# A weight decode of three vector operations instead of four, its low bits made on ScalarE, and a reordered start

## The chip, the core and the metric

One core of a Trainium2 chip runs the whole program. The metric is the device time of one execution in microseconds (us); the time of a kernel is the median of its runs. TensorE multiplies matrices, VectorE (DVE in the rows), ScalarE (ACT) and GpSimd (POOL) work element by element, and SyncE (SP) issues nearly all transfers. TensorE's clock has two levels, 1.2 and 2.4 GHz; the rows give the granted clock as a fraction of 2.4 GHz.

## The reference, cut to what matters

The program takes q, k and v of 4 batches, 8 heads, 576 positions and 64 channels. Each head gets two attentions: one over q, k and v averaged over groups of 4 positions, its result repeated 4 times, and one over the neighbours closer than 4 positions. Their sum, as 2304 tokens of 512 channels, goes through two feed-forward layers whose weights (512 x 2048 and 2048 x 512) come as 64-bit floats.

```python
out_d = sm_attn(q_d, k_d, v_d)             # q_d, k_d, v_d: means over 4 positions
out_up = np.repeat(out_d, factor, axis=2)
...
attn = attn / (np.sum(attn, axis=-1, keepdims=True) + 1e-09)   # masked to |i - j| < 4
out_local = np.matmul(attn, v)
return (out_up + out_local).astype(np.float32)
...
g = h * (1.0 / (1.0 + np.exp(-h)))         # first layer, h = x @ w_in; second: g = elu(h)
return (g @ w_out).astype(np.float32)
```

## The kernel before

**Attention.** Work goes in 16 pairs of heads, and the generator `attention(i)` issues the instructions of one pair piece by piece. A pair's q and k rows are transposed on TensorE (tile `pst`, line 276) and copied by ScalarE. VectorE sums them over groups of 4 (`qkD`, line 289). GpSimd sums the v rows over groups of 4 in three additions (`vt`, line 296, and `vd`, line 297). TensorE then makes the local scores (`psl`, line 308), VectorE adds the mask (line 315) and takes the maximum (`mx`, line 322), GpSimd subtracts it (line 323), ScalarE takes the exponential (line 353), VectorE sums, adds a small constant and inverts (`rl`, lines 355 to 357), and GpSimd multiplies (line 358). The averaged attention goes beside it (lines 334 to 363). Transposes (`aT`, `aD`), products with v (`psu`, `pso`) and a sum into `x32` (line 412) end the pair. The tiles `vt`, `E`, `aT` and `aD` share five buffers of one ring.

**Weights.** A weight tile of 128 x 512 values arrives as 128 x 1024 words in one of three `ws` buffers: the even words are the low halves of the 64-bit floats and the odd words the high halves. `magnitude` lets ScalarE take the absolute value of the high word, read as a float and scaled (line 147). `decode_w` then lets VectorE clamp it (line 156), shift out bits and sign (line 157), put the sign back (line 161) and put the top three bits of the low word into the last places (line 163), after which the next load goes to SyncE's queue (`load_next`). `split_w` makes a rounded high part on ScalarE (line 173) and the rest on GpSimd or VectorE (line 175). 64 weight tiles are decoded in all; the first 16 serve the first pass.

**Order.** Everything is written in one order by hand, and each engine runs its own instructions in that order. A first loop runs pairs 0 to 3 in turn, one piece a step (`step`), counting steps in `n`; in its later steps `small_first` puts in one piece of weight decoding a step, for at most `N_EARLY` = 9 tiles, up to three tiles in turn. The listing gives 82 steps. After it come the units of the matrix products: `g1` (tile `ph`, line 453) and `g2` (tile `y`, lines 504 and 506), with more pieces of attention and decoding at each `tick`; `need_first` forces the two weight tiles that a unit needs. TensorE's products use a high and a low part of both factors. Loads are issued first, in the order in which SyncE's queue runs them.

Of the kernel before, what the change touches and what calls it, by code (L numbers as in the profile page):

```python
# [9 lines left out]
F32 = mybir.dt.float32  # L10
F32R = mybir.dt.float32r
I32 = mybir.dt.int32
BF16 = mybir.dt.bfloat16
AF = mybir.ActivationFunctionType
ALU = mybir.AluOpType
# [6 lines left out]
def attention_moe_moe2_kernel(ctx, tc, q, k, v, wi1, wo1, wi2, wo2, out):  # L22
    nc = tc.nc
    B, H, S, D = q.shape
    NT, DM = out.shape
    DFF = wi1.shape[1]
    P = 128
    FAC = 4
    SD = S // FAC
    HS = SD // 2  # L30
    NPAIR = H // 2
# [12 lines left out]
    EPS = 1e-9  # L44
# [4 lines left out]
    N_EARLY = 9  # L49
# [5 lines left out]
    NW = 10  # L55
# [12 lines left out]
    cpool = ctx.enter_context(tc.tile_pool(name="cpool", bufs=1))  # L68
# [9 lines left out]
    att = attn_pools.enter_context(tc.tile_pool(name="att", bufs=2))  # L78
# [3 lines left out]

    ident = cpool.tile([P, P], F32, name="ident")
    mask = cpool.tile([P, NW // 2, WIN], F32, name="mask")

    def constants():
        make_identity(nc, ident)
        tmp = gp.tile([P, NBM], F32, tag="t", name="masktmp")[:, :4 * WIN].rearrange("p (n w) -> p n w", w=WIN)
        nc.gpsimd.memset(tmp, 0.0)
        for n, (half, low, high) in enumerate([(0, 0, 6), (0, -3, 3), (1, 0, 6), (1, -3, 3)]):  # L90

            for sign, bound in ((1, -low), (-1, high)):
                nc.gpsimd.affine_select(
                    out=tmp[:, n, :], in_=tmp[:, n, :], compare_op=ALU.is_ge, fill=MASKED,
                    base=bound + sign * WIN * half, pattern=[[sign, WIN]], channel_multiplier=-sign,
                )
        for s in range(NW // 2):
            nc.vector.tensor_copy(mask[0:WIN, s, :], tmp[0:WIN, 1 if s == 0 else 0, :])
            nc.vector.tensor_copy(mask[WIN:P, s, :], tmp[WIN:P, 3 if s == NW // 2 - 1 else 2, :])
# [19 lines left out]
    at = {"unit": 0, "load": 0, "decode": 0, "split": 0, "ahead": 2}  # L119

    def load_next():
        if at["load"] < len(order):
            load_w(at["load"])
            at["load"] += 1
# [17 lines left out]
    def magnitude(i):  # L142

        if i < len(order) and i not in wf:
            st = wst[i].rearrange("p (n w) -> p n w", w=2)
            t = wfp[-1].tile([P, DM], I32, tag="wf", name="wf", bufs=wf_bufs[-1])
            nc.scalar.activation(t.bitcast(F32), st[:, :, 1].bitcast(F32), AF.Abs, scale=65536.0)
            wf[i] = t

    def decode_w(i):  # L150
        magnitude(i)
        yield
        st = wst.pop(i).rearrange("p (n w) -> p n w", w=2)
        t = wf[i]
        tf = t.bitcast(F32)
        nc.vector.tensor_scalar(tf, tf, 2.0, W_MAX, op0=ALU.max, op1=ALU.min)  # L156
        nc.vector.tensor_scalar(t, t, 4, 1, op0=ALU.logical_shift_left, op1=ALU.logical_shift_right)  # L157
        yield
        if i + 1 - at["split"] < at["ahead"]:
            magnitude(i + 1)  # L160
        nc.vector.scalar_tensor_tensor(t, st[:, :, 1], -(1 << 31), t, op0=ALU.bitwise_and, op1=ALU.bitwise_or)  # L161
        yield
        nc.vector.scalar_tensor_tensor(t, st[:, :, 0], 29, t, op0=ALU.logical_shift_right, op1=ALU.bitwise_or)  # L163
        load_next()
        yield

# [14 lines left out]
    pairs = [(b, pr) for b in range(B) for pr in range(NPAIR)]  # L181
    loaded = {}
# [5 lines left out]
    def borrow(i, name):  # L188
        at, n = {"qk": (S, 2 * S), "qkD": (3 * S, 2 * SD), "vd": (3 * S + 2 * SD, 2 * SD)}[name]
        return x32[:, pairs[i][1], at:at + n][:, :2 * 2 * D if name == "vd" else n]  # L190

    def load_rows(i, which, engine=None):
        b, h0 = pairs[i][0], 2 * pairs[i][1]
        src = (q, k, v)[which]
        if which == 2:

            if i < NPAIR:
                heads = [wpool.tile([P, DM], F32R, tag=tag, name="rows2").bitcast(F32) for tag in ("wh0", "wl0")]
            else:
                t = nat.tile([P, 4 * FAC * D], F32, tag="natv", name="rows2", bufs=1)  # L200
                heads = [t[:, :DM], t[:, DM:]]
            for j, t in enumerate(heads):
                (engine or nc.sync).dma_start(t[:HS], src[b, h0 + j].rearrange("(p r) d -> p (r d)", r=2 * FAC))
            loaded[i, which] = heads
            return

        if i in (1, 2):
            t = xs.tile([P, KC * NBM], F32R, tag=("xh", "xl")[which], name=f"rows{which}").bitcast(F32)
            borrowed[2 * i - 2 + which] = t
        elif i == 3 and which == 0:  # L210
            borrowed["y"] = yp.tile([P, 4 * NBM], F32, tag="y", name="rows0")
            t = borrowed["y"]
        else:
            t = nat.tile([P, NTB * 2 * D], F32, tag="nat", name=f"rows{which}", bufs=2)
        t = t[:, :NTB * 2 * D].rearrange("p (c e) -> p c e", c=NTB)
        for j in range(2):
            (engine or nc.sync).dma_start(t[:TB, :, j * D:(j + 1) * D], src[b, h0 + j].rearrange("(c p) d -> p c d", p=TB))
        loaded[i, which] = t

    def load_windows(i):  # L220
        b, h0 = pairs[i][0], 2 * pairs[i][1]
        if i in (2, 3):
            vw = borrowed["y"][:, (i - 2) * NW * D:(i - 1) * NW * D].rearrange("p (n d) -> p n d", d=D)
        else:
            vw = nat.tile([P, NW, D], F32, tag="vw", name="vw")
        for j in range(2):
            rows = v[b, h0 + j]
            nc.sync.dma_start(
                vw[j * WIN:(j + 1) * WIN, :NW - 1, :],
                bass.AP(tensor=rows.tensor, offset=rows.offset, ap=[[D, WIN], [w0[1] * D, NW - 1], [1, D]]),  # L230
            )
            nc.sync.dma_start(vw[j * WIN:(j + 1) * WIN, NW - 1, :], rows[w0[-1]:w0[-1] + WIN, :])
        loaded[i, 3] = vw
# [6 lines left out]
    def load_pair(i):  # L240
        for which in range(3):
            load_rows(i, which)
# [15 lines left out]
    def ring(name, n):  # L258
        return att.tile([P, NW * WIN], F32, tag="ring", name=name, bufs=5)[:, :n]

    def attention(i):
# [11 lines left out]
        for parts in ([(0, c) for c in range(NTB - 1)], [(1, c) for c in range(NTB - 1)], [(0, NTB - 1), (1, NTB - 1)]):  # L273
# [3 lines left out]
            o = 0  # L277
            for which in range(2):
                n = TB * sum(w == which for w, _ in parts)
# [7 lines left out]
                    o += n  # L287
            yield
        nc.vector.reduce_sum(qkD, qk.rearrange("p (m r) -> p m r", r=FAC), axis=AX.X)

        vt = ring("vt", 2 * 2 * 2 * D).rearrange("p (n r d) -> p n r d", n=4, r=2)
        vd = borrow(i, "vd") if i < NPAIR else att.tile([P, 4 * D], F32, tag="vd", name="vd", bufs=2)
        vd = vd.rearrange("p (n d) -> p n d", n=4)
        for j, vn in enumerate(loaded.pop((i, 2))):
            vn = vn.rearrange("p (a r d) -> p a r d", a=2, r=FAC)
            nc.gpsimd.tensor_tensor(vt[:HS, 2 * j:2 * j + 2], vn[:HS, :, 0:2, :], vn[:HS, :, 2:4, :], ALU.add)
        nc.gpsimd.tensor_tensor(vd[:HS], vt[:HS, :, 0, :], vt[:HS, :, 1, :], ALU.add)
        if NPAIR - 1 <= i < len(pairs) - 1:
            load_pair(i + 1)
        qT, kT = tT  # L300
        qD, kD = tD

# [2 lines left out]
        for w in range(NW):  # L305
            o = (w % 2) * WIN
# [7 lines left out]
        for j in range(2):  # L314
            nc.vector.scalar_tensor_tensor(
                E[:, :, j, :], psl[j][:, :NW // 2 * WIN].rearrange("p (s w) -> p s w", w=WIN), BSCALE, mask,
                op0=ALU.mult, op1=ALU.add,
# [3 lines left out]
        mx = att.tile([P, NW, 1], F32, tag="mx", name="mx", bufs=4)  # L321
        nc.vector.tensor_reduce(mx, E3, axis=AX.X, op=ALU.max)
        nc.gpsimd.tensor_tensor(E3, E3, mx.to_broadcast([P, NW, WIN]), ALU.subtract)
        if i >= 2:
            load_windows(i)

# [3 lines left out]
        rl = att.tile([P, NW, 1], F32, tag="rl", name="rl", bufs=4)  # L330
# [22 lines left out]
        nc.scalar.activation(E3, E3, AF.Exp)  # L353
        yield
        nc.vector.reduce_sum(rl, E3, axis=AX.X)  # L355
        nc.vector.tensor_scalar_add(rl, rl, EPS)  # L356
        nc.vector.reciprocal(rl, rl)
        nc.gpsimd.tensor_tensor(E3, E3, rl.to_broadcast([P, NW, WIN]), ALU.mult)

# [174 lines left out]
    with tc.manual_schedule():  # L534
        for i in range(NPAIR):
            load_rows(i, 0)
            load_rows(i, 1, nc.scalar if i < 2 else nc.sync)
        for i in range(NPAIR):
            if i == 2:
                while at["load"] < 3:  # L540
                    load_next()
            load_rows(i, 2)
        load_windows(0)
        load_windows(1)

        zeros = gp.tile([P, NBM], F32, tag="t", name="zeros")
        nc.vector.memset(zeros, 0.0)
# [97 lines left out]
        while pending(0):  # L645
            step()

            while done < NPAIR and state["next"] > done and pairs[done] not in [p for p, _, _ in state["live"]]:
                next(first_x)
                done += 1  # L650
            n += 1
            if n <= 16:
                warm(1)
            if n > 36 and first["next"] < N_EARLY:
                small_first()
        del banks[1:]
        banks[0] = (ps_a, "a")
# [103 lines left out]
```

## Time and profile before

| | |
|---|---|
| median of 3 runs | 991.67 us (991.29 to 991.95) |
| the profiled execution | 991.21 us, its span 989.4 us |
| TensorE busy | 956.6 us (97%) |
| VectorE busy | 563.5 us (57%) |
| ScalarE busy | 412.4 us (42%) |
| GpSimd busy | 372.7 us (38%) |

The span runs from the first to the last instruction of the profiled execution. Busy time counts an instruction from its start to its end, so an instruction that has started and stands still counts as busy. Line numbers are those of the listing above. "Idle before" is the idle time of the engine just ahead of an instruction, and the arrow names what ended it.

### The profile page before, as it was taken

To read this page: it belongs to the slowest core of one execution; us is meant where nothing else is said; L and a number is where in the kernel's file an instruction comes from. 1 tells how busy PE (TensorE), PEld (TensorE's weight loads), DVE (VectorE), ACT (ScalarE), POOL (GpSimd) and SP (SyncE) were. 2 spreads that over 40 slices of the span, in tenths; PEclk is the share of its full clock that TensorE was granted. 3 is DMA by queue.
4 is the path that set the end of the run, shared out by engine and by line. 5 is a ranking of instruction groups with operands and counts; after the bars stand their busy time and mean duration, and the time that the engine had idled before them with its cause. 6 is when DMAs were issued, how large, how long until landed. Compare 5 with 4: busy or idle time off the path is not lost.

```text
span 989.4 us, 18693 instructions
## 1 busy us (share of the span) xinstructions
PE 956.6 (97%) x7453; PEld 884.8 (89%) x7453; DVE 563.5 (57%) x1012; ACT 412.4 (42%) x1032; POOL 372.7 (38%) x391
## 2 busy tenths in 40 slices
PE   7787799999999999999999999999999999999998
PEld 4566689999999999999999999999999999999997
DVE  6899955364479938766232367677644544334432
ACT  4455444545445456443333454433333433223321
POOL 4556755464422354222222362222223622222221
PEclk9758899999999999999999999999999999999999
DMA  9465553333125512434000101222000011101111
GB/s 219 106 167 134 155 129 75 97 84 89 36 86 162 167 57 86 129 109 127 23 22 24 43 1 54 86 96 64 33 33 32 1 64 65 63 2 64 64 36 60
DMA packets 90582, 77.74 MB, mean 79 GB/s; under 512 B 61568, under 2 KB 77952, under 8 KB 90496
## 3 DMA queue, kind: packets, MB, share of 16 engines
q1 hardware_dynamic: 88128, 75.97, 26.5%
q8 instruction: 58, 0.95, 0.4%
q10 hardware_dynamic: 2368, 0.59, 0.3%
q14 instruction: 28, 0.23, 0.1%
HBM read 62.39 MB, written 14.16 MB: 77 GB/s over the span
## 4 chain that ended last, share of the span: by engine, by line
PE 88%; DVE 8%; issue 1%; ACT 1%; DMA 1%; POOL 1%; SPq 0%; DVEq 0%; POOLq 0%; ACTq 0%
PE ph L453 41%; PE y L504 21%; PE y L506 20%; PE pso L404 2%; PE pst L276 1%; DVE wf L163 1%; DVE wf L161 1%; PE psu L392 1%; PE psl L308 1%; DVE wf L156 1%; PE psE L375 1%; PE psD L384 1%; DVE wf L157 1%; DVE rl L356 1%; DVE rl L355 1%
## 5 line engine op out<-in xcount | busy, mean ns | idle before, releaser
L476 POOL TENSOR_TENSOR gl<-t,gh 128x256 fp32r<-128x256 f32 (+1 forms) x240 | 218.0, 908 | 532.5 <-ACT gh L474 517.6
L453 PE MATMUL ph<-xl,wh 128*128 128x256 f32 (+1 forms) x960 | 278.6, 308 | 4.5 <-DVE xl L433 4.5
L453 PE MATMUL ph<-xh,wh 128*128 128x256 f32 (+1 forms) x960 | 278.6, 308 | 0.4 <-DVE t L466 0.4
L453 PEld LDWEIGHTS ph<-xl,wh 128*128 128x128 f32 x960 | 183.3, 191 | 9.7 <-DVE xl L433 4.9
L453 PEld LDWEIGHTS ph<-xh,wh 128*128 128x128 f32 x960 | 183.4, 191 | 7.0 <-issue 1.6
L453 PE MATMUL ph<-xh,wl 128*128 128x256 f32 (+1 forms) x960 | 178.6, 305 | 1.4 <-POOL wl L175 1.4
L504 PE MATMUL y<-gh,wh 128*128 128x256 f32 x576 | 168.9, 293 | 0.0
L474 ACT CAST gh<-t 128x256 fp32r<-128x256 f32 (+1 forms) x240 | 108.0, 450 | 139.6 <-DVE t L466 90.1
L504 PE MATMUL y<-gh,wl 128*128 128x256 f32 x576 | 164.5, 286 | 0.0
L504 PE MATMUL y<-gl,wh 128*128 128x256 f32 x576 | 164.5, 286 | 0.0
L466 DVE SCALAR_TENSOR_TENSOR t<-t,ph 128x256 f32<-128x256 f32 x144 | 60.3, 419 | 165.5 <-ACT t L464 165.5
L453 PEld LDWEIGHTS ph<-xh,wl 128*128 128x128 f32 x960 | 148.7, 191 | 2.3 <-POOL wl L175 1.6
L470 ACT ACTIVATE t<-t 128x384 f32<-128x384 f32 x96 | 50.4, 526 | 210.7 <-DVE t L469 210.7
L469 DVE TENSOR_SCALAR t<-ph 128x384 f32<-128x384 f32 x96 | 53.4, 556 | 125.6 <-PE ph L453 125.5
L506 PE MATMUL y<-wl,gh 128*128 128x512 f32 x288 | 113.9, 396 | 0.0
L464 ACT ACTIVATE t<-ph 128x256 f32<-128x256 f32 x144 | 55.3, 384 | 140.3 <-PE ph L453 131.5
L506 PE MATMUL y<-wh,gl 128*128 128x512 f32 x288 | 113.7, 395 | 0.0
L504 PEld LDWEIGHTS y<-gh,wh 128*128 128x128 f32 x576 | 111.8, 194 | 1.9 <-issue 1.0
L504 PEld LDWEIGHTS y<-gh,wl 128*128 128x128 f32 x576 | 112.0, 194 | 0.0
L504 PEld LDWEIGHTS y<-gl,wh 128*128 128x128 f32 x576 | 112.0, 194 | 0.0
L506 PE MATMUL y<-wh,gh 128*128 128x512 f32 x288 | 111.9, 389 | 0.0
L472 DVE SCALAR_TENSOR_TENSOR t<-t,ph 128x384 f32<-128x384 f32 x96 | 53.2, 554 | 56.8 <-ACT t L470 56.8
(85 smaller groups left out, 1241.8 us busy)
## 6 DMA issues: line engine op xcount, KB each, us to landing
ws<-in_moe_w_in_dram SPq DMA_DIRECT2D x32, 512.0 KB
ws<-in_moe_w_out_dram SPq DMA_DIRECT2D x32, 512.0 KB
rows<-in_v_dram SPq DMA_DIRECT2D x36, 144.0 KB
rows<-in_q_dram SPq DMA_DIRECT2D x32, 144.0 KB
yp<-yo SPq DMA_DIRECT2D x9, 512.0 KB
part<-yp SPq DMA_DIRECT2D x9, 512.0 KB
yp<-yo SPq DMA_DIRECT2D x6, 768.0 KB
part<-yp SPq DMA_DIRECT2D x6, 768.0 KB
```

What stands on the lines that cost most here:

```text
L156: nc.vector.tensor_scalar(tf, tf, 2.0, W_MAX, op0=ALU.max, op1=ALU.min)
L404: nc.tensor.matmul(ps[j * D:(j + 1) * D, o:o + n], loaded[i, 3][j * WIN:(j + 1) * WIN, w, :], aT[j * WIN:(j + 1) * WIN, w // 2, c0:c0 + n] ...
L453: nc.tensor.matmul(ph[:, :nb], a[:, c, :], b[:, c, :], start=k == 0, stop=k == 3 * KC - 1)
L464: nc.scalar.activation(t, h, AF.Tanh, scale=0.5)
L466: nc.vector.scalar_tensor_tensor(t, t, 1.0, h, op0=ALU.add, op1=ALU.mult)
L469: nc.vector.tensor_scalar_min(t, h, 0.0)
L470: nc.scalar.activation(t, t, AF.Exp)
L472: nc.vector.scalar_tensor_tensor(t, t, -1.0, h, op0=ALU.add, op1=ALU.max)
L474: nc.scalar.copy(gh, t)
L476: nc.gpsimd.tensor_tensor(gl, t, gh.bitcast(F32), ALU.subtract)
L504: nc.tensor.matmul(y[d // 2][:, h:h + nb], wm[:, sl], gm, start=first and d % 2 == 0, stop=last, skip_group_check=True)
L506: nc.tensor.matmul(y[d], gm[:, sl], wm, start=first, stop=last)
```

## The change

Five things are edited. ScalarE gets a second instruction for each weight tile, right behind the absolute value: it reads the low word as an unsigned integer, scales it by 2^-29 with an offset and writes the rounded result, the three bits, back over the low word. VectorE's shift becomes one operation that shifts the clamped value left by 3 and puts in these bits; the fourth operation goes, and with it one break (`yield`) in `decode_w`. The sums of v on GpSimd, and the loads of the next pair that follow them, move from ahead of the local scores to behind the subtraction of the maximum. The constant added to `rl` comes from a tile `eps` through a `tensor_tensor`. The first weight loads move ahead of the v rows, in turn with them and with the v windows, and the first loop begins to decode at every second step from step 13 on, where it was every step from step 37 on.

```diff
--- before.py
+++ after.py
@@ -10,6 +10,7 @@
 F32 = mybir.dt.float32
 F32R = mybir.dt.float32r
 I32 = mybir.dt.int32
+U32 = mybir.dt.uint32
 BF16 = mybir.dt.bfloat16
 AF = mybir.ActivationFunctionType
 ALU = mybir.AluOpType
@@ -82,9 +83,11 @@
 
     ident = cpool.tile([P, P], F32, name="ident")
     mask = cpool.tile([P, NW // 2, WIN], F32, name="mask")
+    eps = cpool.tile([P, 1], F32, name="eps")
 
     def constants():
         make_identity(nc, ident)
+        nc.gpsimd.memset(eps, EPS)
         tmp = gp.tile([P, NBM], F32, tag="t", name="masktmp")[:, :4 * WIN].rearrange("p (n w) -> p n w", w=WIN)
         nc.gpsimd.memset(tmp, 0.0)
         for n, (half, low, high) in enumerate([(0, 0, 6), (0, -3, 3), (1, 0, 6), (1, -3, 3)]):
@@ -145,6 +148,8 @@
             st = wst[i].rearrange("p (n w) -> p n w", w=2)
             t = wfp[-1].tile([P, DM], I32, tag="wf", name="wf", bufs=wf_bufs[-1])
             nc.scalar.activation(t.bitcast(F32), st[:, :, 1].bitcast(F32), AF.Abs, scale=65536.0)
+
+            nc.scalar.activation(st[:, :, 0].bitcast(U32), st[:, :, 0].bitcast(U32), AF.Copy, scale=2.0 ** -29, bias=2.0 ** -10 - 0.5)
             wf[i] = t
 
     def decode_w(i):
@@ -154,13 +159,11 @@
         t = wf[i]
         tf = t.bitcast(F32)
         nc.vector.tensor_scalar(tf, tf, 2.0, W_MAX, op0=ALU.max, op1=ALU.min)
-        nc.vector.tensor_scalar(t, t, 4, 1, op0=ALU.logical_shift_left, op1=ALU.logical_shift_right)
+        nc.vector.scalar_tensor_tensor(t, t, 3, st[:, :, 0], op0=ALU.logical_shift_left, op1=ALU.bitwise_or)
         yield
         if i + 1 - at["split"] < at["ahead"]:
             magnitude(i + 1)
         nc.vector.scalar_tensor_tensor(t, st[:, :, 1], -(1 << 31), t, op0=ALU.bitwise_and, op1=ALU.bitwise_or)
-        yield
-        nc.vector.scalar_tensor_tensor(t, st[:, :, 0], 29, t, op0=ALU.logical_shift_right, op1=ALU.bitwise_or)
         load_next()
         yield
 
@@ -287,16 +290,6 @@
                     o += n
             yield
         nc.vector.reduce_sum(qkD, qk.rearrange("p (m r) -> p m r", r=FAC), axis=AX.X)
-
-        vt = ring("vt", 2 * 2 * 2 * D).rearrange("p (n r d) -> p n r d", n=4, r=2)
-        vd = borrow(i, "vd") if i < NPAIR else att.tile([P, 4 * D], F32, tag="vd", name="vd", bufs=2)
-        vd = vd.rearrange("p (n d) -> p n d", n=4)
-        for j, vn in enumerate(loaded.pop((i, 2))):
-            vn = vn.rearrange("p (a r d) -> p a r d", a=2, r=FAC)
-            nc.gpsimd.tensor_tensor(vt[:HS, 2 * j:2 * j + 2], vn[:HS, :, 0:2, :], vn[:HS, :, 2:4, :], ALU.add)
-        nc.gpsimd.tensor_tensor(vd[:HS], vt[:HS, :, 0, :], vt[:HS, :, 1, :], ALU.add)
-        if NPAIR - 1 <= i < len(pairs) - 1:
-            load_pair(i + 1)
         qT, kT = tT
         qD, kD = tD
 
@@ -321,6 +314,16 @@
         mx = att.tile([P, NW, 1], F32, tag="mx", name="mx", bufs=4)
         nc.vector.tensor_reduce(mx, E3, axis=AX.X, op=ALU.max)
         nc.gpsimd.tensor_tensor(E3, E3, mx.to_broadcast([P, NW, WIN]), ALU.subtract)
+
+        vt = ring("vt", 2 * 2 * 2 * D).rearrange("p (n r d) -> p n r d", n=4, r=2)
+        vd = borrow(i, "vd") if i < NPAIR else att.tile([P, 4 * D], F32, tag="vd", name="vd", bufs=2)
+        vd = vd.rearrange("p (n d) -> p n d", n=4)
+        for j, vn in enumerate(loaded.pop((i, 2))):
+            vn = vn.rearrange("p (a r d) -> p a r d", a=2, r=FAC)
+            nc.gpsimd.tensor_tensor(vt[:HS, 2 * j:2 * j + 2], vn[:HS, :, 0:2, :], vn[:HS, :, 2:4, :], ALU.add)
+        nc.gpsimd.tensor_tensor(vd[:HS], vt[:HS, :, 0, :], vt[:HS, :, 1, :], ALU.add)
+        if NPAIR - 1 <= i < len(pairs) - 1:
+            load_pair(i + 1)
         if i >= 2:
             load_windows(i)
 
@@ -353,7 +356,7 @@
         nc.scalar.activation(E3, E3, AF.Exp)
         yield
         nc.vector.reduce_sum(rl, E3, axis=AX.X)
-        nc.vector.tensor_scalar_add(rl, rl, EPS)
+        nc.vector.tensor_tensor(rl, rl, eps.rearrange("p (n o) -> p n o", o=1).to_broadcast([P, NW, 1]), ALU.add)
         nc.vector.reciprocal(rl, rl)
         nc.gpsimd.tensor_tensor(E3, E3, rl.to_broadcast([P, NW, WIN]), ALU.mult)
 
@@ -535,13 +538,12 @@
         for i in range(NPAIR):
             load_rows(i, 0)
             load_rows(i, 1, nc.scalar if i < 2 else nc.sync)
+        load_next()
         for i in range(NPAIR):
-            if i == 2:
-                while at["load"] < 3:
-                    load_next()
             load_rows(i, 2)
-        load_windows(0)
-        load_windows(1)
+            if i < 2:
+                load_windows(i)
+                load_next()
 
         zeros = gp.tile([P, NBM], F32, tag="t", name="zeros")
         nc.vector.memset(zeros, 0.0)
@@ -651,7 +653,7 @@
             n += 1
             if n <= 16:
                 warm(1)
-            if n > 36 and first["next"] < N_EARLY:
+            if n > 12 and n % 2 and first["next"] < N_EARLY:
                 small_first()
         del banks[1:]
         banks[0] = (ps_a, "a")
```

## Rows read from the trace of the kernel before

**Rows 1.** Busy time by stretch: microseconds and instructions of each engine, granted clock, DMA.
```profile
0.00:34.00 34.00, 23.60 (x292) 14.16 (x293) 20.95 (x42) 13.78 (x47) 19.54 (x34) 0.97 0.92 199
34.00:70.00 36.00, 30.44 (x305) 22.04 (x302) 32.95 (x56) 18.70 (x50) 17.59 (x15) 0.59 0.48 128
70.00:130.00 60.00, 46.94 (x472) 41.37 (x472) 57.31 (x89) 31.60 (x94) 45.22 (x37) 0.84 0.64 156
130.00:990.00 860.00, 855.58 (x6389) 807.22 (x6388) 452.33 (x827) 348.28 (x843) 290.33 (x307) 1.00 0.21 66
```

**Rows 2.** Chain that ended last, shares by line: 53 to 64 us, 64 to 131 us.
```profile
by line: PE psu L392 23.2%; PE pso L404 22.8%; PE pst L276 17.4%; PE psE L375 13.9%; PE psD L384 11.6%; PE psl L308 11.4%; issue 0.4%
...
by line: DVE wf L163 13.7%; issue 12.2%; DVE wf L161 9.4%; DVE wf L156 8.5%; DVE xl L433 7.1%; DVE wf L157 4.9%; DVE E L315 4.5%; DVE mx L322 4.5%; DVE qkD L289 4.0%; DVE t L466 3.6%; DVE x L412 3.4%; DVE rl L355 3.3%; DVE nm L343 3.3%; ACT
```

**Rows 3.** Instructions by line, VectorE, first 130 us: count, busy, mean ns, idle before.
```profile
L163 DVE SCALAR_TENSOR_TENSOR wf<-ws,wf 128x512 int32<-128x512 int32 x16 | 16.3, 1029 | 0.0
L157 DVE TENSOR_SCALAR wf<-wf 128x512 int32<-128x512 int32 x16 | 15.3, 958 | 0.6
L161 DVE SCALAR_TENSOR_TENSOR wf<-ws,wf 128x512 int32<-128x512 int32 x16 | 14.6, 918 | 0.0
L156 DVE TENSOR_SCALAR wf<-wf 128x512 f32<-128x512 f32 x16 | 10.8, 674 | 6.3 <-ACT wf L147 6.3
...
L433 DVE TENSOR_TENSOR xl<-x,xh 128x256 fp32r<-128x256 f32 x8 | 6.3, 794 | 0.0
...
L356 DVE TENSOR_SCALAR rl<-rl 128x10 f32<-128x10 f32 x7 | 5.2, 747 | 0.2
```

**Rows 4.** Timeline, 28 to 60 us: start, length, engine, line; POOL is GpSimd.
```profile
35.11 0.43 DVE L157 TENSOR_SCALAR wf<-wf 128x512 int32<-128x512 int32 x1
35.57 0.69 DVE L161 SCALAR_TENSOR_TENSOR wf<-ws,wf 128x512 int32<-128x512 int32 x1
...
37.87 1.67 POOL L323 TENSOR_TENSOR E<-E,mx 128x640 f32<-128x640 f32 x1 [4.96 <-DVE mx L322]
...
38.45 1.37 DVE L157 TENSOR_SCALAR wf<-wf 128x512 int32<-128x512 int32 x1
```

**Rows 5.** Timeline, 126 to 131 us, one subtraction on VectorE among GpSimd instructions.
```profile
126.89 1.28 POOL L175 TENSOR_TENSOR wl<-wf,wh 128x512 fp32r<-128x512 f32 x1
126.94 2.77 DVE L433 TENSOR_TENSOR xl<-x,xh 128x256 fp32r<-128x256 f32 x1
...
128.14 1.25 POOL L323 TENSOR_TENSOR E<-E,mx 128x640 f32<-128x640 f32 x1
```

**Rows 6.** Busy time of the instructions on tile wf alone, two stretches.
```profile
34.00:70.00 36.00, 22.47 (x27) 9.06 (x14) 7.99 (x6) 0.59 0.48 128
70.00:130.00 60.00, 33.43 (x37) 11.24 (x18) 13.79 (x10) 0.84 0.64 156
```

**Rows 7.** Timeline of the first 30 us, the softmax of the first pairs.
```profile
9.78 0.82 DVE L322 TENSOR_REDUCE mx<-E 128x10 f32<-128x640 f32 x1
...
14.95 1.41 POOL L296 TENSOR_TENSOR vt<-rows 72x256 f32<-72x256 f32 x2 [11.25 <-DMA rows<-in_v_dram]
...
17.12 1.26 POOL L323 TENSOR_TENSOR E<-E,mx 128x640 f32<-128x640 f32 x1
...
18.41 0.74 ACT L353 ACTIVATE E<-E 128x640 f32<-128x640 f32 x1 [3.07 <-POOL E L323]
...
20.03 1.76 DVE L356 TENSOR_SCALAR rl<-rl 128x10 f32<-128x10 f32 x1
```

**Rows 8.** DMA of the first 60 us in 40 slices, rate of each.
```profile
GB/s 0 149 264 213 214 215 215 220 224 254 266 339 364 243 178 184 122 96 109 109 134 228 235 104 11 115 332 129 4 0 0 0 104 407 188 0 0 61 296 3
```

**Rows 9.** Waits of the first 130 us: in total, times, longest.
```profile
DVE wf L156 <- ACT wf L147: 6.3, 4, 3.8
ACT aD L385 <- POOL x L297: 6.2, 1, 6.2
```

**Rows 10.** Instructions by line, ScalarE, first 130 us.
```profile
L147 ACT ACTIVATE wf<-ws 128x512 f32<-128x512 f32 x16 | 10.8, 676 | 4.5 <-POOL wl L175 4.2 <-DMA ws<-in_moe_w_out_dram 0.3
```

## Prediction

> **What bounds the kernel now.** I read the busy times by stretch first [rows 1]. From 130 us on TensorE is busy for 855.58 of 860 us at a granted clock of 1.00, the 2.4 GHz level, and the few idle microseconds are the tail. Nothing that this change does can shorten that stretch, because the products in it stay the same. So the time is about 860 us plus the moment at which this regime begins, and the question is only how much earlier than 130 us that is. Before it TensorE has 10.4 idle us up to 34, 5.6 from 34 to 70 and 13.1 from 70 to 130, and its clock is 0.59 and 0.84 in the last two.
>
> Next is what those 130 us wait for. VectorE is busy for 32.95 of 36 and 57.31 of 60 us in the two later stretches [rows 1]. The chain that ended last [rows 2] runs from 64 to 131 us mostly through the decode's lines 163, 161, 156 and 157. Between 53 and 64 us, however, it is TensorE alone, with the attention's products at a clock of 0.5, the 1.2 GHz level.
>
> VectorE's busy time is not all work [rows 3, 4]. With GpSimd idle the shift took 0.43 us and the next operation 0.69 us. The shift at 38.45 us took 1.37 us: GpSimd's subtraction had begun at 37.87 us for 1.67 us, and the shift ended 0.28 us behind it. So this shift stands while GpSimd works, and its mean is 958 ns. The operations with two tensors do the same: at 126.94 us a `tensor_tensor` took 2.77 us, through two GpSimd instructions, and ended just behind the second [rows 5]. From 34 to 130 us the decode's 64 VectorE operations hold 55.9 us [rows 6], where their undisturbed lengths (two at 0.43, two at 0.69) come to 16 x 2.24 = 35.8 us. About 20 us are waiting, 0.31 us an operation.
>
> **The decode after the first loop.** Of the 64 operations 27 lie in 34 to 70 us and 37 in 70 to 130 us [rows 6]. A step of the first loop that decodes moves one of up to three tiles on by one piece, with seven pieces to a tile before and six after. Counting them through to step 82, the new order leaves 28 of 48 operations behind it, where the old left 37 of 64: the same share, so the same nine weight tiles are still to do. Nine operations go. Lower bound of the gain: the operation that goes is a shift in effect (one shift and one combination become one combination), 0.43 us undisturbed, and all the waiting moves to the other three, because GpSimd's work does not shrink: 9.25 x 0.43 = 4.0 us. Upper bound: each of the nine takes its full mean with it, 33.43 x 9/37 = 8.1 us. GpSimd is busy for 45.22 of the 60 us, so part of the waiting will come back. I take the middle, **6.0 us**.
>
> **The decode within the loop.** Steps 13 to 36 now hold eight decode operations that stood behind step 36; steps 37 to 82 hold 12 instead of 27. At the old mean (22.47/27 = 0.83 us) VectorE loses 12.5 us of its 32.95. The stage can't shrink by that: TensorE is idle for only 5.6 of its 36 us at this clock, and it is the chain for 11 us of it [rows 1, 2]. Bounds: 0 and 5.6 us at the same clock, more only if the clock rises. I take **5.0 us**, near the idle time, since the waits ahead of 53 us are VectorE's and GpSimd's.
>
> **The start.** Now GpSimd's first work is the first v sum at 14.95 us, behind an 11.25 us wait for v rows, and the first subtraction comes at 17.12 us, although its maximum was ready at 10.6 us; ScalarE's exponential waits 3.07 us for it [rows 7]. The move frees that subtraction. It does not free the second: in GpSimd's queue it stands behind the first v sum, and so do all the later ones. That v sum now waits longer, since one weight load of 0.52 MB passes the first v rows; at the 266 to 364 GB/s of the slices in which the loads ran [rows 8] this is 1.4 to 2.0 us. On ScalarE the absolute values of tiles 0, 1 and 2 stand at steps 13, 17 and 23, ahead of transposes and exponentials of pairs 1 to 3. The second load is queued behind 2.36 MB of q and k, the first load, one v pair (0.29 MB) and its windows (0.33 MB): 4.0 MB in all with itself; the slices sum to that at about 18.5 us, where ScalarE would come to it at about 17. The third needs 1.15 MB more, at about 23 us. What is queued behind each wait is all of ScalarE's attention work, and TensorE waits for its copies. Against this, VectorE is idle for 13 of the first 34 us [rows 1], so the eight operations (6.7 us at the old mean) find room there, though GpSimd's 19.54 busy us in this stretch will lengthen them [rows 1]. The ring helps: ScalarE waited 6.2 us for the last v sum before `aD` got its buffer [rows 9], and this v sum is now allocated later than that `aD`. Bounds: no loss, and 6 us (three stalls of 2 us). I take a loss of **2.5 us**.
>
> **ScalarE's new instruction.** No row shows it. Nearest is line 147, the same 128 x 512 with the same two-word stride, mean 676 ns [rows 10]. 16 of them cost ScalarE about 11 us in the first 130 us, where it is idle for about half. It is hidden by that, and by VectorE's clamp, which needs only the absolute value and runs 0.43 us meanwhile. Uncovered it costs its length wherever VectorE already waited for ScalarE: four times, 6.3 us in all [rows 9]. Bounds 0 and 4 x 0.68 = 2.7 us; I take **1.0 us**. Behind 130 us the 48 others are covered by TensorE.
>
> **The sum's constant.** Line 356 takes 747 ns on the mean over 10 elements, once 1.76 us [rows 3, 7]. As a `tensor_tensor` it reads two tensors, and rows 5 show such an operation standing behind GpSimd too. The Trainium skill, page "SBUF — State Buffer", section "Who interferes with whom", says that a VectorE instruction with two SBUF inputs contends with a GpSimd instruction that reads SBUF, and that only instructions with one input outside the two-port modes are free. By that rule this edit frees nothing, and the trace agrees with the 2.77 us of [rows 5]. Even if it did, line 360, a `tensor_scalar`, comes two instructions later. Bounds: 0, and 7 x 0.747 = 5.2 us if it came to cost nothing at all. I take **0**.
>
> **Loads later on.** The next pair's loads stand in SyncE's queue behind a later v sum, so a weight load behind them can come later by the two GpSimd instructions in between, some 2 us a pair. Weight loads wait for free buffers anyway; I take 0, at most 2 us.
>
> **Sum** against the profiled execution of 991.21 us: -6.0 - 5.0 + 2.5 + 1.0 = -7.5, or 983.7 us. The median is 0.46 us above that execution, so I predict **984.2 us**. A difference under 0.2% (2 us) can't be told from none here.
>
> **Rivals.** (1) *GpSimd sets the pace.* All waiting returns: 4.0 us after the loop, 7 x 0.43 = 3.0 within it, less 3.5: about 988.2 us. For it speaks GpSimd's 45.22 us; against it that this busy time also holds waiting for VectorE. (2) *The stages overlap better.* With VectorE light, TensorE stays busy, its clock rises in 34 to 70 us, and VectorE's whole 12.5 us count there for 9, with 8.1 after the loop and nothing lost at the start: about 975 us. Against it: that stage had a clock of 0.59. (3) *Slower: ScalarE stands at the loads.* If the waits at steps 17 and 23 last 6 to 7 us each (loads land late, as the first v rows did after 11.25 us of waiting), the start loses 13 instead of 2.5 us: 994.7 us. It decides from a start loss of 10 us on. Against it: the rates of [rows 8]. (4) *No change*: TensorE at the low clock holds 34 to 70 us and the start eats the rest: -4.0 + 3.5, about 991 us.
>
> **How the numbers follow.** My forecast (981 to 987.5 us) has 0.45, rival 1 (to 989.6) 0.13, rival 2 (below 981) 0.20, no change 0.08, slower 0.14. Faster: 0.45 + 0.13 + 0.20 = 0.78. The range 976 to 990.5 us leaves out the far end of rival 2, rival 3 and half of rival 4.
>
> **What would show it.** Right: TensorE's last long wait ends 6 to 9 us before 130 us; 48 VectorE decode operations for the first 16 tiles in about 45 us; ScalarE waits of about 2 us for `ws` at 15 to 25 us; line 356 still over 1 us where GpSimd works; the first subtraction near 11 us. Wrong: a first product of tile `ph` later than 68 us, a new ScalarE instruction above 1 us, or waits of VectorE for ScalarE well above 6.3 us.

## The result, and the profile after

The changed kernel takes 1001.87 us in the median (999.95 to 1004.7, four runs) against 991.48 us before: a ratio of 1.011, with a 95% interval of 1.0078 to 1.0142. It is slower, where 984.2 us was forecast and 976 to 990.5 us was the range. The slowest execution before (991.95 us) and the fastest after (999.95 us) lie 8 us apart. Its profiled execution took 1000.22 us, with a span of 998.4 us, 9.0 us above that of before.

Busy time by stretch of the kernel after, which answers to [rows 1]:

```profile
0.00:34.00 34.00, 24.53 (x282) 14.73 (x282) 23.07 (x41) 16.48 (x48) 17.20 (x30) 0.85 1.06 196
34.00:70.00 36.00, 27.24 (x312) 19.60 (x312) 30.35 (x50) 20.08 (x57) 19.06 (x18) 0.67 0.54 124
70.00:130.00 60.00, 43.81 (x430) 38.29 (x430) 47.58 (x71) 33.93 (x91) 39.03 (x34) 0.77 0.57 145
130.00:998.00 868.00, 860.91 (x6437) 810.92 (x6433) 434.96 (x789) 376.65 (x900) 300.82 (x313) 1.00 0.22 67
```

From 130 us on, TensorE is busy for 860.91 us where it was 855.58: 5.3 us more of its work is left at that moment. It is also idle for 7.1 us there, where it was 4.4. VectorE did get lighter, 47.58 instead of 57.31 us from 70 to 130, but TensorE was busy for 3.1 us less in that same stretch, with a granted clock of 0.77 where it had been 0.84. The engine that had been busiest there was relieved, and the work that counts fell behind.

The decode's part of these rows, by the instructions on tile `wf` alone (VectorE, ScalarE and GpSimd), answers to [rows 6]:

```profile
0.00:34.00 34.00, 8.97 (x8) 2.64 (x4) 1.46 (x1) 0.85 1.06 196
34.00:70.00 36.00, 12.16 (x13) 5.73 (x9) 5.07 (x4) 0.67 0.54 124
```

VectorE had no decode up to 34 us before. So its other work there fell from 20.95 to 23.07 - 8.97 = 14.10 us, and from 34 to 70 us it rose from 32.95 - 22.47 = 10.48 to 30.35 - 12.16 = 18.19 us. The early decode did not only fill idle time: it went in ahead of other work, which came later.

A marker for how far behind is ScalarE's sixteenth reading of `ph`. One instruction by its tile, before and then after; the last time in each line (169.6 and 173.9 us) is the start of the sixteenth:

```profile
L464 ACT ACTIVATE t<-ph x16: 372/384/402, 74.5 to 169.6; 128x256 f32<-128x256 f32 x16
```
```profile
L467 ACT ACTIVATE t<-ph x16: 377/385/413, 76.5 to 173.9; 128x256 f32<-128x256 f32 x16
```

So 4.3 of the 9.0 us are lost by this point, and the other 4.7 us behind it. Behind it TensorE has 5890 instructions (5891 before); it is idle for 7.5 us where it was 3.8, and busy for 817.03 us where it was 815.98. The idle part, 3.6 us, is TensorE's waits of the kernel after from 160 us on, which are new (before had 0.2 us in all there); the 1.1 us of longer busy time stay open:

```profile
PE pst L279 <- ACT ED L351: 1.4, 1, 1.4
PE ph L456 <- DVE t L469: 1.1, 1, 1.1
PE pst L279 <- DMA rows<-in_q_dram: 1.1, 1, 1.1
PE psu L395 <- ACT aD L388: 0.2, 1, 0.2
```

VectorE's instructions by line in the first 140 us, after, answering to [rows 3]:

```profile
L162 DVE SCALAR_TENSOR_TENSOR wf<-wf,ws 128x512 int32<-128x512 int32 x16 | 21.3, 1331 | 1.1
L166 DVE SCALAR_TENSOR_TENSOR wf<-ws,wf 128x512 int32<-128x512 int32 x16 | 16.2, 1018 | 0.0
L161 DVE TENSOR_SCALAR wf<-wf 128x512 f32<-128x512 f32 x16 | 13.6, 847 | 5.8 <-ACT wf L150 5.8
...
L363 DVE TENSOR_SCALAR sm<-sm 72x4 f32<-72x4 f32 x7 | 3.7, 527 | 0.0
L359 DVE TENSOR_TENSOR rl<-rl,eps 128x10 f32<-128x10 f32 x7 | 2.8, 400 | 0.2
```

The 48 operations take 51.1 us, where 64 took 57.0 and about 45 was forecast. Each that is left takes longer, the new L162 1331 ns on the mean. With the decode alone (*e1_decode*, below) the 48 take 45.0 us, as forecast, and the new operation 1071 ns.

ScalarE's two instructions for a tile, same stretch, answering to [rows 10]:

```profile
L150 ACT ACTIVATE wf<-ws 128x512 f32<-128x512 f32 x16 | 10.8, 674 | 7.2 <-DMA ws<-in_moe_w_in_dram 5.1 <-DMA ws<-in_moe_w_out_dram 2.1
L152 ACT ACTIVATE ws<-ws 128x512 uint32<-128x512 uint32 x16 | 10.6, 664 | 0.0
```

The new one takes 664 ns, as long as the row that bounded it. But ScalarE now stands 7.2 us for weight loads, where the old listing had 0.3.

Timeline of the kernel after, 10 to 30 us, answering to [rows 7]:

```profile
10.69 1.26 POOL L316 TENSOR_TENSOR E<-E,mx 128x640 f32<-128x640 f32 x1 [6.96 <-DVE mx L315]
...
17.32 0.72 POOL L323 TENSOR_TENSOR vt<-rows 72x256 f32<-72x256 f32 x1 [5.37 <-DMA rows<-in_v_dram]
18.13 0.66 ACT L150 ACTIVATE wf<-ws 128x512 f32<-128x512 f32 x1 [3.23 <-DMA ws<-in_moe_w_in_dram]
...
22.50 0.67 ACT L150 ACTIVATE wf<-ws 128x512 f32<-128x512 f32 x1 [2.07 <-DMA ws<-in_moe_w_out_dram]
...
28.00 0.68 ACT L150 ACTIVATE wf<-ws 128x512 f32<-128x512 f32 x1 [1.88 <-DMA ws<-in_moe_w_in_dram]
```

The first subtraction came at 10.69 us, as forecast. The first v sum came at 17.32 us, 2.4 us later than before, and the three waits of ScalarE for its loads are 3.23, 2.07 and 1.88 us.

Finally a wait that no row of before has. Timeline of the kernel after, 75 to 94 us (SPq is SyncE's queue):

```profile
75.91 0.51 SPq L139 DMA_DIRECT2D ws<-in_moe_w_out_dram  x1
...
84.99 0.40 SPq L134 DMA_DIRECT2D ws<-in_moe_w_in_dram  x1
...
86.38 0.92 SPq L220 DMA_DIRECT2D rows<-in_q_dram  x2
...
93.15 1.04 PE L279 MATMUL pst<-ident,rows 96*128 96x96 f32 x5 [4.88 <-DMA rows<-in_q_dram]
```

and the same pair's loads before:

```profile
71.70 0.36 SPq L136 DMA_DIRECT2D ws<-in_moe_w_out_dram  x1
77.03 0.40 SPq L131 DMA_DIRECT2D ws<-in_moe_w_in_dram  x1
77.55 0.97 SPq L217 DMA_DIRECT2D rows<-in_q_dram  x2
```

After, the queue stood with a weight load until 84.99 us, when a `ws` buffer came free, and the q rows were behind it and one more. They left 8.8 us later than before, and TensorE stood 4.88 us for them.

### The profile page after: what moved, and what is told of

It reads as the page before. It is cut to its first block, busy times and chain, and to the rows that moved or that the text cites. A ratio compares the mean times of both kernels' runs of the same rounds, so it can differ in the third digit from the quotient of the medians.

```text
span 998.4 us, 18706 instructions
## 1 busy us (share of the span) xinstructions
PE 956.5 (96%) x7453; PEld 883.5 (88%) x7453; DVE 536.0 (54%) x948; ACT 447.1 (45%) x1096; POOL 376.1 (38%) x392
## 4 chain that ended last, share of the span: by engine, by line
PE 65%; DMA 1%; DVE 0%; ACT 0%; issue 0%; SPq 0%
PE ph L456 33%; PE y L509 20%; PE y L507 13%; DMA ws<-in_moe_w_in_dram 0%; DMA ws<-in_moe_w_out_dram 0%; DVE part L530 0%; ACT ws L152 0%; DVE wf L166 0%; DVE wf L162 0%; ACT t L467 0%; DVE t L469 0%; DVE wf L161 0%; ACT wf L150 0%; SPq L134 0%
## 5 line engine op out<-in xcount | busy, mean ns | idle before, releaser
L479 POOL TENSOR_TENSOR gl<-t,gh 128x256 fp32r<-128x256 f32 (+1 forms) x240 | 220.7, 920 | 525.9 <-ACT gh L477 507.8
```

Source lines behind the costliest of these rows:

```text
L479: nc.gpsimd.tensor_tensor(gl, t, gh.bitcast(F32), ALU.subtract)
```

## The experiments

Each kernel was timed beside the kernel before on its own chip (990.65 to 991.24 us there); the ratio is to that, with its 95% interval. Differences between medians of different chips are sure only to about 0.6 us.

### The parts by themselves

*e1_decode*: the kernel before with the hunks of `magnitude` and `decode_w` alone.

```diff
+ nc.scalar.activation(st[:, :, 0].bitcast(U32), ..., AF.Copy, scale=2.0 ** -29, bias=...)
- nc.vector.tensor_scalar(t, t, 4, 1, ...)
+ nc.vector.scalar_tensor_tensor(t, t, 3, st[:, :, 0], ...)
- yield
- nc.vector.scalar_tensor_tensor(t, st[:, :, 0], 29, t, ...)
```

> The kernel before with the three-operation decode and ScalarE's low bits alone. Theory Q (the moved loads are the loss: with the v sums the next pair's q, k and v loads go later in SyncE's queue, and products and weight loads wait for them): this part is a gain, 983 to 989 us. Theory S (ScalarE is the loss: the second instruction of each tile lengthens its in-order queue): 993 to 999 us.

Measured: 987.26 us, 0.996 (0.9946 to 0.9975). The decode by itself gains 4.0 us, as theory Q has it.

*e2_vsum*: before with the v sums and `load_pair(i + 1)` behind the subtraction, nothing else.

> The kernel before with only the v sums, and the loads that follow them, behind the maximum. Theory Q: this is the loss, 996 to 1003 us, with TensorE waiting for q rows and SyncE waiting for the v sum for over 10 us between 60 and 140 us. Theory S: nothing on ScalarE changes, 989 to 993 us.

Measured: 991.04 us, 1.0 (0.999 to 1.0009). No difference alone, against theory Q. Its first product of `ph` comes at 60.0 us, 6.7 us earlier than before, and nothing of that is left at the end.

*e3_start*: before with the two start hunks.

```diff
+        load_next()
         for i in range(NPAIR):
-            if i == 2:
-                while at["load"] < 3:
-                    load_next()
             load_rows(i, 2)
-        load_windows(0)
-        load_windows(1)
+            if i < 2:
+                load_windows(i)
+                load_next()
...
-            if n > 36 and first["next"] < N_EARLY:
+            if n > 12 and n % 2 and first["next"] < N_EARLY:
```

> The kernel before with only the new order of the first loads and decoding from step 13 on at every second step; decode and v sums as before. Theory Q: 989 to 994 us. Theory S (ScalarE waits for weight loads at steps 13, 17 and 23, ahead of the attention): 994 to 999 us.

Measured: 997.06 us, 1.0063 (1.0042 to 1.0085): the reordered start loses 5.8 us (five executions, 994.24 to 1000.52), as theory S has it.

*e4_no_vsum*: the changed kernel with the v sums and the loads at their old place.

> The changed kernel with the v sums and the loads behind them put back ahead of the local scores. Theory Q: the loss goes and the decode's gain is left, 983 to 990 us, no wait of TensorE for q rows after 60 us. Theory S: 999 to 1003 us.

Measured: 995.88 us, 1.0047 (1.0032 to 1.0062). The start costs 8.6 us on top of decode and constant (987.32, below). The time lies between the ranges of both theories: neither is the whole of it.

### What in the start costs

*e6_load_order* and *e7_pace* are before with one hunk of e3_start each; *e14_decode_load_order* and *e15_decode_pace* are e1_decode with the same.

> The kernel before with only the new order of the first loads. If the start's loss is the load order (v rows later for GpSimd): 994 to 998 us. If it is the decoding at every second step from step 13 on: 990 to 993 us.

> The kernel before with only decoding from step 13 on at every second step, the first loads in the old order. If the pacing is the loss (ScalarE stands at the first weight loads ahead of the attention, and fewer tiles are ready at the loop's end): 994 to 1000 us. If the load order is: 990 to 993 us.

> Three-operation decode and the new load order, old pacing. If the late v rows delay GpSimd and with it the attention whatever the decode does (the load order alone cost 3.2 us): 990 to 992 us. If the load order costs only with the early decoding: 987 to 989 us.

> Three-operation decode and decoding from step 13 on at every second step, old load order. If the pacing's loss grows with ScalarE's second instruction at the loads (alone it cost 1 us): 990 to 993 us. If it only leaves fewer tiles ready at the loop's end, 5 instead of 6: 988 to 990 us.

| | load order | pacing |
|---|---|---|
| on before | 994.19 us, 1.0035 (1.0023 to 1.0048) | 992.03 us, 1.0017 (1.0006 to 1.0027) |
| on e1_decode | 991.3 us, 1.0012 (1.0001 to 1.0022) | 992.22 us, 1.0023 (1.0013 to 1.0032) |

The load order costs 3.2 us on before and 4.0 on e1_decode, the pacing 1.0 and 5.0 (992.22 - 987.26). The first two came out as expected if the load order is the loss, the third as if it costs whatever the decode does, the fourth as if the pacing's loss grows on the decode. For the load order the first v sum of e6_load_order, timeline:

```profile
17.57 0.72 POOL L296 TENSOR_TENSOR vt<-rows 72x256 f32<-72x256 f32 x1 [13.88 <-DMA rows<-in_v_dram]
```

With this edit alone the wait of 11.25 us at 14.95 us [rows 7] became one of 13.88 us, and GpSimd's waits for v rows from 9 to 45 us grew from 11.2 to 16.7 us. The loss lies ahead of the matrix products: on e1_decode the first product of `ph` comes at 69.40 instead of 65.97 us, and from there to the sixteenth reading of `ph` both kernels take 98.3 us.

For the pacing, the instructions on tile `wf` from the start to the first product of `ph`. The columns are VectorE, ScalarE and GpSimd; before, after, decode with the old pacing (e10_decode_eps, below) and e7_pace:

```profile
0.00:66.60 66.60, 21.23 (x26) 8.44 (x13) 7.71 (x6) 0.77 0.68 161
```
```profile
0.00:66.90 66.90, 19.64 (x18) 8.37 (x13) 6.54 (x5) 0.74 0.79 161
```
```profile
0.00:65.60 65.60, 18.68 (x21) 8.95 (x14) 8.40 (x6) 0.77 0.74 168
```
```profile
0.00:64.00 64.00, 21.04 (x22) 6.54 (x10) 5.03 (x4) 0.81 0.72 159
```

GpSimd's last step has been done for 6 tiles with the old pacing, for 5 in the changed kernel and for 4 in e7_pace. The code says why: every step from 37 to 82 is 46 pieces, every second step from 13 on is 35. It starts earlier and does less. In e7_pace, whose first product comes at 64.09 us, TensorE then stood for the weights (its waits from 62 us on):

```profile
PE ph L453 <- ACT wh L173: 9.6, 3, 5.6
PE ph L453 <- POOL wl L175: 5.2, 2, 4.0
```

Before has 1.4 us of this kind, all of it on `wl`. Other waits became shorter, so that TensorE's idle time from the first product to the sixteenth reading grew by 3.0 us only (18.6 against 15.5).

On the decode, where the pacing costs 5.0 us, no product of `ph` waits for `wh` or `wl` there. The same stretch, e1_decode and then e15_decode_pace, columns as in the first table:

```profile
66.00:164.30 98.30, 84.05 (x978) 75.16 (x977) 68.50 (x126) 56.60 (x170) 59.24 (x58) 0.93 0.57 135
```
```profile
65.50:169.40 103.90, 88.62 (x977) 78.63 (x976) 72.08 (x129) 57.46 (x171) 62.16 (x58) 0.87 0.54 131
```

The first product comes 0.5 us earlier with the new pacing, and the stretch is 5.6 us longer. So the loss does not lie at ScalarE's waits in the loop, which the first expectation of e15_decode_pace named, though the time is in its range. TensorE was busy for 4.6 us longer with the same work, at a granted clock of 0.87 instead of 0.93, and idle for 1.0 us longer. Up to 80 us it was busy for 7.75 of 14.5 us at 0.72, where e1_decode has 11.14 of 14.0 us at 0.88; it stood 4.1 us for VectorE's `xl` there instead of 1.4. The kernel after has 88.55 us of busy time at 0.87 for the same products. That all this follows from the one tile less fits, but was not shown.

### What the v sums do with the rest

*e8_no_start*: the changed kernel with the old start. *e9_split*: decode and v sums, with only the v load of the next pair behind its v sum. *e5_qk_loads_back*: the changed kernel with that same edit.

```diff
         nc.vector.reduce_sum(qkD, ...)
+        if NPAIR - 1 <= i < len(pairs) - 1:
+            for which in range(2):
+                load_rows(i + 1, which)
...
-            load_pair(i + 1)
+            load_rows(i + 1, 2)
```

> The changed kernel with the old first loads and the old pacing: three-operation decode, moved v sums, constant from a tile. If the parts add up (decode -4, v sums 0): 986 to 989 us. If the moved v sums need the start's order to lose: below 986 us is possible, the decode gaining on top of an attention that ends 6 us earlier. If the v sums lose 6 us whatever the start: 992 to 995 us.

> The kernel before with the three-operation decode and the moved v sums, old start, old constant; the next pair's q and k loads stay ahead of the local scores, its v load behind the v sum. In the changed kernel with the old start TensorE waited 16.2 us for q rows. If these waits are what the v sums cost: 975 to 984 us, and no wait for q rows. If GpSimd's order itself costs it: 989 to 993 us.

> The changed kernel with the next pair's q and k loads put back ahead of the local scores; its v load stays behind the v sum. If the v sum's move costs what it does because these loads start late (TensorE waited 6.7 us for q rows in the changed kernel): 994 to 997 us and no such wait. If it costs through GpSimd's order instead: 1000 to 1003 us.

Measured: e8_no_start 991.62 us, 1.0011 (0.9999 to 1.0023); e9_split 987.38 us, 0.9971 (0.9962 to 0.9981); e5_qk_loads_back 997.63 us, 1.0067 (1.0052 to 1.0082). The late q and k loads cost 4.2 us between the first two, whose intervals are apart (e8_no_start also has the constant from `eps`, which costs nothing by itself, below). All three times fell between the ranges that were expected. In the changed kernel they cost 4.2 us by the medians, but 2.0 us by the profiled spans (996.4 against 998.4), with intervals that touch. TensorE's waits of e8_no_start from 65 us on:

```profile
PE pst L279 <- DMA rows<-in_q_dram: 16.2, 3, 8.9
PE pst L279 <- ACT ED L351: 2.8, 3, 1.4
```

The wait for q rows is the largest, in the changed kernel too (6.7 us from 65 us on); before and e5_qk_loads_back have none, e9_split has 0.6 us. The second line is another consequence: with the moved v sums ScalarE stands for GpSimd's `vd` before it writes `ED`. ScalarE's waits of the kernel after from 160 to 580 us:

```profile
ACT ED L351 <- POOL vd L324: 6.4, 5, 2.3
```

e9_split has 5.7 us of this wait; before and e16_first_pairs (below), with the old order of the later pairs, have none. That it comes from the shared ring, in which the move changes the order of `vt`, was not tested.

### What an operation is worth

*e10_decode_eps*: e1_decode with the constant from `eps`. *e12_act_only*: before with the new ScalarE instruction, its result unused and overwritten by the absolute value, and all four VectorE operations; here the new instruction stands ahead of the absolute value, in the change behind it. *e13_no_low*: before without the fourth operation and its `yield`; it leaves the last three bits of each weight at zero.

```diff
e10  + nc.vector.tensor_tensor(rl, rl, eps..., ALU.add)
e12  + nc.scalar.activation(t.bitcast(U32), st[:, :, 0].bitcast(U32), AF.Copy, ...)
e13  - nc.vector.scalar_tensor_tensor(t, st[:, :, 0], 29, t, ...)
```

> The three-operation decode and the constant from a tile, nothing else. If the tile's tensor_tensor only moves the wait to the next tensor_scalar: 986 to 989 us, as the decode alone. If that moved wait costs (the next tensor_scalar stood 3.07 us in the changed kernel): 989 to 993 us.

> The kernel before with one more ScalarE instruction for each weight tile: it makes the low bits into the tile that the absolute value then writes over, so nothing uses them; VectorE keeps its four operations. If ScalarE's instruction is hidden: 990 to 992 us. If it costs the 1 to 2.7 us that the prediction bounds: 992 to 994 us.

> The kernel before with VectorE's fourth decode operation left out, so the last three bits of each weight stay zero; ScalarE does nothing more. The decode without its price on ScalarE. If one operation a tile is worth the 6 to 12 us of the prediction: 979 to 985 us. If GpSimd sets the pace: 985 to 989 us.

Measured: e10_decode_eps 987.32 us, 0.9969 (0.9958 to 0.998), as e1_decode and as expected if the constant changes nothing. e12_act_only 994.1 us, 1.0041 (1.0026 to 1.0056): ScalarE's instruction costs 3.2 us with nothing in return, just above the range that was expected if it is not hidden, and in an order that also makes VectorE's clamp wait for it. By the profiled executions (2.9 us) 1.6 us of this are lost by the sixteenth reading of `ph` (171.2 against 169.6 us), as much as VectorE's waits for `wf` grew (7.9 against 6.3 us), and 1.3 us behind it (821.1 against 819.8 us to the end). e1_decode has 821.3 us there. e13_no_low 981.75 us, 0.9917 (0.9898 to 0.9935): the operation that goes is worth 9.2 us, all of it by the sixteenth reading (160.2 against 169.6 us). This is in the range that was expected if an operation is worth 6 to 12 us. -9.2 + 3.2 = -6.0, and e1_decode has -4.0. The 2.0 us between are of the size of the third difference, a shift of 0.43 us that became an operation of 0.69 us [rows 4]: 16 x 0.26 = 4.2 us undisturbed. Up to 130 us the three operations take 45.0 us in e1_decode and 42.6 us in e13_no_low, 2.4 us more. That the difference is this was not measured by itself.

### A version that keeps the gains

*e16_first_pairs*: e1_decode, and the v sums behind the subtraction for pairs 0 to 3 alone; loads and ring order of the later pairs as before. *e17_first_pairs_more*: the same, decoding at every step from 29 on.

```diff
+        if i >= NPAIR: vd = vsums()      # at the old place
...
+        if i < NPAIR: vd = vsums()       # behind the subtraction
e17:
-            if n > 36 and first["next"] < N_EARLY:
+            if n > 28 and first["next"] < N_EARLY:
```

> Three-operation decode; v sums behind the maximum for pairs 0 to 3 alone, all loads at their old places. If the earlier end of the loop (6 us with the moved v sums) is worth something once the later pairs are left alone: 981 to 985 us. If the decode behind the loop takes it all back: 986 to 988 us.

> The same with decoding in every step from step 29 on (it was 37). If the decode behind the loop is what bounds and the loop has room: 977 to 984 us. If the early tiles displace attention as in the changed kernel: 986 to 992 us.

Measured: e16_first_pairs 984.84 us, 0.9947 (0.9932 to 0.9962), in its first range and the fastest that keeps the whole computation; e17_first_pairs_more 985.97 us, 0.9955 (0.9939 to 0.9972), between its ranges and no different. The interval of e16_first_pairs overlaps that of e1_decode (0.9946 to 0.9975), so that the early v sums add to the decode's gain is likely and not sure. e9_split, which moves the v sums of all pairs, takes 2.5 us longer; the two intervals meet at 0.9962. TensorE's waits of e16_first_pairs from 160 us on, without q rows and without `ED`:

```profile
PE ph L461 <- DVE t L474: 1.0, 1, 1.0
PE psu L400 <- ACT aD L393: 0.2, 1, 0.2
```

## Why the prediction was wrong

By medians the way from 991 to 1001.9 us is: decode and constant to 987.3 (e10_decode_eps), the v sums without the q and k loads to 987.4 (e9_split), those loads to 991.6 (e8_no_start), the start to 1001.9. Against the forecast, decode and ScalarE's instruction gave 3.6 us (e10_decode_eps against its own before) instead of 10.0, the loads cost 4.2 instead of 0, and the start 10.2 instead of 2.5. These gaps sum to 18.3 us; the forecast missed by 17.7. None of the three signs of being wrong showed in the kernel after (first product at 66.99 us, 664 ns, 5.8 us of VectorE's waits for ScalarE's `wf`): they watched the loop and ScalarE, and the first product was only 0.3 us late: nearly all of the loss lay behind it.

**The decode within the loop (-5.0): failed.** The argument was that VectorE loses 12.5 us of its load from 34 to 70 us, because the operations moved ahead find room in the first 34 us, and that the stage shrinks by its idle time. The count held: 13 decode operations are left there where 12 were forecast, and they take 10.3 us less (12.16 against 22.47). But 7.7 us of other work came in from ahead, so VectorE lost only 2.6 us (30.35 against 32.95), and the first product of `ph` came at 66.99 us, where it had been 66.67. The pacing alone does this in part: in e7_pace VectorE's other work up to 34 us is 23.06 - 7.08 = 16.0 us, where it was 20.95. The second error is behind the loop. What I compared was the share of operations left behind (28 of 48 forecast, 30 measured) with the old share, and called it "the same nine weight tiles". The comparison that mattered was with keeping the old pacing, which leaves 27 of 48 and one tile more that is finished. The pacing costs 5.0 us on the decode, most of it as the longer busy time of TensorE shown above; why the clock was lower there stays open. In the sum above this price is a part of the start's 10.2.

**The start (+2.5, bounds 0 and 6).** The mechanism was right: v rows later, and ScalarE standing at three loads. The sizes were not. The three stalls are 7.2 us, a little over the upper bound; the second and third load let ScalarE go on at 22.50 and 28.00 us, where 18.5 and 23 were forecast, so they landed later than the rates of [rows 8] gave. The load order costs 3.2 to 4.0 us, without any decode in the early steps. Order and pacing together cost 5.8 us on before, 8.6 on the decode and 10.2 with all other edits; they come to more together with the rest than apart, and what they do to each other was not taken apart further. Rival 3 had the right sign, and the start's 10.2 us are past the 10 us from which it was to decide, but it went by waits of 6 to 7 us each, which did not come.

**Loads later on (0, at most 2 us): failed.** The step looked at the weight loads behind the q and k loads. It was the other way round: the q and k loads came to stand behind a weight load that waits for a buffer, and TensorE needs them. This costs 4.2 us between e9_split and e8_no_start.

**The decode after the loop (-6.0) and ScalarE's instruction (+1.0).** Right in sign. The operation was worth 9.2 us in e13_no_low, within the sum of the bounds (4.0 to 8.1 behind the loop, 0 to 5.6 in it); the whole decode, with the longer operation in place of the shift and ScalarE's part, gained 4.0. The chain that was called mostly the decode's has 36.5% on its four lines [rows 2]. The ScalarE term was mis-sized: 3.2 us in e12_act_only, above its upper bound of 2.7, though in an order harder on VectorE than that of the change. Its bound counted VectorE's four waits for `wf`, and those grew by 1.6 us. It took the 48 instructions behind 130 us as covered by TensorE; behind the sixteenth reading they cost 1.3 us in e12_act_only.

**The constant (0): right.** e10_decode_eps equals e1_decode. The new L359 has a mean of 491 ns there, and the old form of the same line in e1_decode 496; the fall from 747 [rows 3] came with the decode and not with this edit. The next `tensor_scalar` stays at 103 ns. In the kernel after it rose to 527 (L363), which thus comes with the other edits. The Trainium skill, page "SBUF — State Buffer", section "Who interferes with whom", states that a VectorE instruction with two SBUF inputs contends with a GpSimd instruction that reads SBUF, and the new form has two; the unchanged mean and time agree that the edit frees nothing.

## What to carry to other kernels

A new pacing must be compared with the old pacing of the same new code, and not by its share of the work: look at what is ready when it is needed, and at what the early pieces push back. Idle time of an engine in a stretch is no proof that more work fits in without delaying the rest. When a statement moves down in the program, list every DMA issue that moves with it and what is then ahead of it in its queue: a load that waits for a buffer holds all behind it. An idle half of an engine is no sure cover for a new instruction on it: ask what others wait for that is queued behind that instruction.

## What the runs showed of the hardware

One 128 x 512 VectorE operation for each of 16 tiles, with an undisturbed length of 0.69 us (11.0 us in all) and a mean of 1.03 us beside GpSimd (16.3 us), was worth 9.2 us when it went without replacement (e13_no_low). So its own mean was not what removing it gave back.

How long the decode's operations stand beyond their undisturbed lengths was not set by their number. For the first 16 tiles it was 57.0 - 35.8 = 21.2 us before, 45.0 - 29.0 = 16.0 us in e1_decode, and 51.1 - 29.0 = 22.1 us in the kernel after, which has the same operations as e1_decode in another order of the start and of the v sums.

The same stretch of TensorE's work (978 and 977 instructions in the traces) held it busy for 84.05 us at a mean granted clock of 0.93 and for 88.62 us at 0.87 (e1_decode and e15_decode_pace).
